# Gated linear attention before a mixture of experts: chunk steps for all head pairs at once, three fp32r passes for the query-key products

## The chip, the cores and the metric

One core of a Trainium2 chip runs the kernel. The metric is the device time of one execution in microseconds (us).

## The reference

Three stages follow each other. The inputs are random; N = 4 * 768 = 3072 tokens, 8 heads of 48 channels, 4 experts.

```python
f = 1 / (1 + exp(-f_logit))                              # [4, 8, 768, 48]
for t in range(768):
    state = f[:, :, t, :, None] * state + k_t (outer) v_t   # per head 48 x 48
    y[:, :, t] = q_t @ state
x = y as [3072, 384]
out = sum over e of p[:, e] * (relu(x @ w1[e]) @ w2[e])     # 384 -> 1024 -> 384
result = ((out @ u1) * (out @ u2)) @ u3 @ uo               # 384 -> 1024 -> 1024 -> 384
```

## The kernel before

The recurrence is computed in chunks of C = 128 tokens. Inside a chunk a running product of 1 + exp(-f_logit), `pi`, is made by a scan; the key is multiplied by `pi`, the query by its reciprocal `r`, and then attention within the chunk is an ordinary masked product, to which the query times the `state` carried from earlier chunks is added. Heads go in NP = 4 pairs; a pair fills R = 96 partitions (48 channels of one head above 48 of the other).

The elementwise part, called prep here (`attn_f` to `attn_q`, L204 to L252), works on one pair and NB = 384 tokens at a time: clamp (L207), exp (L211), add 1 (L218, or L213 on ScalarE for the first four), three scans of 128 columns (L222), ln and exp for the reciprocal (L233, L234), two VectorE instructions that refine it (L241, L242), key and query products on GpSimd (L236, L247). GpSimd also makes `qb` (L258), the query once for each head of a pair with the other head's rows zeroed, so that one matmul over 96 rows gives both heads.

The tensor part, `attn_s` (L273), takes one slot, which is one chunk of one pair; there are 96 slots. TensorE does a transpose of k (L287), the query-key product of 256 columns (L288), the state update `u` (L295) and two or three products for y (L299, L300, L302), all in plain fp32, where a matmul is two passes; the profile counts each pass as an instruction. y leaves TensorE with channels on partitions and is split into a high fp32r part (ScalarE, L334) and the rest (VectorE, L336) in `x`. Slot k does the query-key part of slot k and the y part of slot k - 1.

The expert stage works in units: one expert, one block of 512 tokens, 128 hidden columns. `stage1` is 9 fp32r matmuls (L642), ScalarE and VectorE split their result into high and low (`hid`, L648, L649), and `stage2` is 9 more matmuls (L676) of the unit before. Weights are loaded in chunks of 768 columns and split by `split_chunk` (ScalarE L168, GpSimd L169). The first block's units come in halves of 256 tokens: units 0 to 7 need the first two chunks of attention, units 8 to 15 the first four. A last part (kind "M") does the gated product stage with the same two lines.

The order of everything is written out: each attention step has a due time, the list is sorted, steps up to the eighth slot run before the first unit (that is two chunks, `K0`), and `spread` lays the others over the units by planned time; within a unit the first half of its steps is issued after `stage1` and the other half after `stage2`. Every engine runs its instructions in that order. Loads are issued on SP's queue in the same order.

Of the kernel before, what the change touches and what calls it, by code (L numbers as in the profile page):

```python
# [24 lines left out]
def gated_linear_attention_moe_kernel(  # L25
# [21 lines left out]
    NB = 384  # L47
# [10 lines left out]
    CB = TB // C  # L58

# [10 lines left out]
    fp = ctx.enter_context(tc.tile_pool(name="fp", bufs=3))  # L70
    kqp = ctx.enter_context(tc.tile_pool(name="kqp", bufs=6))
    vtp = ctx.enter_context(tc.tile_pool(name="vtp", bufs=3))
    atp = ctx.enter_context(tc.tile_pool(name="atp", bufs=3))
    qbp = ctx.enter_context(tc.tile_pool(name="qbp", bufs=3))
# [4 lines left out]
    ps_a = ctx.enter_context(tc.tile_pool(name="ps_a", bufs=3, space=PSUM))  # L79
# [19 lines left out]
    def setup():  # L99
# [3 lines left out]
        nc.vector.memset(capt, CAP)  # L103
        nc.vector.memset(cmask, 1.0)
# [9 lines left out]
        nc.vector.tensor_scalar(  # L114
            out=hm[:, 1:2], in0=hm[:, 0:1], scalar1=-1.0, scalar2=1.0, op0=ALU.mult, op1=ALU.add
# [3 lines left out]
    def gate_load():  # L119
        t = const.tile([128, NTILE, E], F32, name="praw")  # L120
        nc.scalar.dma_start(out=t, in_=probs)
        return t
# [8 lines left out]
    def gate_rows(t):  # L131
        ps = ps_a.tile([128, 512], F32, tag="at", name="pT")
# [121 lines left out]
    def attn_b(n, c):  # L254
# [783 lines left out]
```

## Time and profile before

| | |
|---|---|
| median of 3 runs | 1332.62 us (1332.45 to 1333.32) |
| the profiled execution's own time | 1333.76 us |
| its span from first to last instruction | 1332.0 us |
| TensorE / VectorE / ScalarE / GpSimd busy | 1291.6 / 706.3 / 458.8 / 606.0 us |
| mean granted TensorE clock | 0.987 of 2.4 GHz |
| matmuls of the expert and the gated stage (L642, L676) | 41% and 34% of the chain that ended last |
| first attention matmul / first expert matmul / first of unit 8 | 22.95 / 37.00 / 87.90 us from the start |

Busy time counts an instruction from its start to its end; TensorE instructions overlap, so what one costs is the distance from its start to the next one's start. In the profile's names PE is TensorE, PEld its weight load, DVE VectorE, ACT ScalarE, POOL GpSimd.

### The profile page before, as it was taken

What the parts mean: (1) busy time and instruction counts of PE and PEld (TensorE: products, weight loads), DVE (VectorE), ACT (ScalarE), POOL (GpSimd) and SP (SyncE); (2) the same over time, 40 slices, a digit from 0 to 9 for tenths busy, and PEclk for the clock granted to TensorE, in tenths of its full rate; (3) what the DMA queues carried; (4) which work ended last, traced back from release to release, by engine and by line L of the source; (5) the groups of instructions that cost most, each with busy time, mean ns of one, the idle gap of its engine ahead of it and who ended that gap; (6) DMA issues with size and microseconds to landing.
All of it is one profiled execution on the core that took longest, in us unless ns stands there. A gap on an engine that the chain in (4) does not pass through costs nothing.

```text
span 1332.0 us, 17861 instructions
## 1 busy us (share of the span) xinstructions
PE 1291.6 (97%) x6579; PEld 1125.9 (85%) x6579; DVE 706.3 (53%) x1365; ACT 458.8 (34%) x946; POOL 606.0 (45%) x573
## 2 busy tenths in 40 slices
PE   7689999999999999999999999999999999999997
PEld 6588888888887888888788878878888999999997
DVE  6765545445546766665634776767733233332422
ACT  4434424333332423323222332323323334433431
POOL 6656736575354444636354353635625132233310
PEclk8889999999999999999999999999999999999999
DMA  6424224323133252424032241333313323241301
GB/s 190 150 65 143 92 56 145 101 73 112 65 108 126 80 147 77 134 78 143 26 112 103 78 130 53 109 103 97 95 49 118 102 78 113 73 130 55 113 1 39
DMA packets 75584, 128.49 MB, mean 96 GB/s; under 512 B 6528, under 2 KB 48992, under 8 KB 75488
## 3 DMA queue, kind: packets, MB, share of 16 engines
q1 hardware_dynamic: 75344, 127.21, 30.8%
q8 instruction: 54, 0.88, 0.3%
q14 instruction: 42, 0.34, 0.1%
q10 hardware_dynamic: 144, 0.05, 0.0%
HBM read 113.03 MB, written 14.20 MB: 96 GB/s over the span
## 4 chain that ended last, share of the span: by engine, by line
PE 86%; DVE 7%; POOL 2%; issue 2%; ACT 2%; DMA 1%; SPq 0%; POOLq 0%; ACTq 0%; DVEq 0%
PE hps L642 41%; PE y L676 34%; PE psP L288 3%; PE wps L555 2%; PE psQ L299 1%; PE psQ L300 1%; PE psQ L302 1%; DVE pi L222 1%; PE psP L295 1%; POOL acc L696 1%; DVE hid L649 1%; DMA f<-in_fkq_dram 1%; DVE dexp L474 1%; POOL w L169 1%; DVE dexp L473 1%
## 5 line engine op out<-in xcount | busy, mean ns | idle before, releaser
L642 PE MATMUL hps<-x,w 128*128 128x512 f32 (+2 forms) x2952 | 647.4, 366 | 2.6 <-ACT x L334 1.4
L642 PEld LDWEIGHTS hps<-x,w 128*128 128x128 f32 x2952 | 529.4, 189 | 73.0 <-ACT x L334 1.8
L676 PE MATMUL y<-hid,w 128*128 128x512 f32 (+1 forms) x1800 | 445.4, 391 | 10.9 <-DVE hid L649 5.8
L169 POOL TENSOR_TENSOR w<-raw,w 128x768 fp32r<-128x768 f32 x160 | 299.0, 1870 | 263.3 <-ACT w L168 243.6
L676 PEld LDWEIGHTS y<-hid,w 128*128 128x128 f32 x1800 | 329.2, 191 | 82.6 <-DVE hid L649 8.9
L649 DVE SCALAR_TENSOR_TENSOR hid<-hps,hid 128x512 fp32r<-128x512 f32 (+1 forms) x200 | 133.5, 668 | 331.1 <-ACT hid L648 330.7
L648 ACT ACTIVATE hid<-hps 128x512 fp32r<-128x512 f32 (+1 forms) x200 | 115.4, 577 | 293.7 <-PE hps L642 285.1
L168 ACT ACTIVATE w<-raw 128x768 fp32r<-128x768 f32 x160 | 133.9, 837 | 34.4 <-PE y L676 30.7
L656 DVE TENSOR_TENSOR ab<-hps,a 128x384 f32<-128x384 f32 x64 | 35.6, 556 | 164.2 <-PE hps L642 164.2
L493 POOL TENSOR_TENSOR dman<-dman,dexp 128x384 f32<-128x384 f32 (+1 forms) x46 | 46.1, 1003 | 161.2 <-ACT dman L491 154.8
L676 PE MATMUL y<-w,hid 128*128 128x384 f32 x576 | 112.1, 338 | 0.1
L676 PEld LDWEIGHTS y<-w,hid 128*128 128x128 f32 x576 | 101.7, 188 | 0.5 <-DVE hid L658 0.4
L696 POOL TENSOR_TENSOR acc<-acc,tmp 128x512 f32<-128x512 f32 x54 | 70.1, 1326 | 60.7 <-DVE tmp L695 60.7
L340 POOL TENSOR_TENSOR state<-us,pwe 96x96 f32<-96x96 f32 x80 | 28.5, 357 | 127.4 <-DVE us L308 66.5
L491 ACT ACTIVATE dman<-dman 128x384 f32<-128x384 f32 (+1 forms) x46 | 23.9, 520 | 145.8 <-DVE dman L490 130.1
L657 ACT ACTIVATE hid<-ab 128x384 fp32r<-128x384 f32 x64 | 33.6, 525 | 114.9 <-DVE ab L656 114.9
L288 PE MATMUL psP<-qb,kq 96*128 96x256 f32 x180 | 56.5, 396 | 5.2 <-POOL state L340 3.9
L258 POOL TENSOR_TENSOR qb<-kq,hm 96x256 f32<-96x256 f32 x90 | 57.4, 641 | 5.0 <-PE psP L288 5.0
L312 ACT ACTIVATE kT<-psQ 128x96 f32<-128x96 f32 x80 | 19.9, 248 | 111.5 <-PE psQ L302 79.2
L655 ACT ACTIVATE a<-hps 128x384 f32<-128x384 f32 x64 | 31.4, 490 | 77.9 <-PE hps L642 77.2
L336 DVE TENSOR_TENSOR x<-psQ,x 96x128 fp32r<-96x128 f32 (+1 forms) x144 | 41.0, 285 | 28.2 <-ACT x L334 26.9
L658 DVE TENSOR_TENSOR hid<-ab,hid 128x384 fp32r<-128x384 f32 x64 | 35.7, 558 | 37.8 <-ACT hid L657 37.8
(92 smaller groups left out, 1147.8 us busy)
## 6 DMA issues: line engine op xcount, KB each, us to landing
raw<-in_w_dram SPq DMA_DIRECT2D x112, 384.0 KB, 4.2
raw<-in_u_dram SPq DMA_DIRECT2D x27, 384.0 KB, 4.0
kq<-in_fkq_dram SPq DMA_DIRECT2D x30, 288.0 KB, 4.1
vt<-in_vp_dram SPq DMA_DIRECT2D x24, 288.0 KB, 3.1
pb<-pdr SPq DMA_DIRECT2D x24, 256.0 KB, 5.2
raw<-u1d SPq DMA_DIRECT2D x16, 384.0 KB, 3.5
raw<-u2d SPq DMA_DIRECT2D x16, 384.0 KB, 3.6
raw<-wdr SPq DMA_DIRECT2D x16, 384.0 KB, 3.9
```

Source lines behind the costliest of these rows:

```text
L168: nc.scalar.activation(out=w[:, 0], in_=raw, func=AF.Copy)
L169: nc.gpsimd.tensor_tensor(out=w[:, 1], in0=raw, in1=w[:, 0].bitcast(F32), op=ALU.subtract)
L258: nc.gpsimd.tensor_tensor(out=qb, in0=q.unsqueeze(1).to_broadcast([R, 2, C]), in1=hm.unsqueeze(2).to_broadcast([R, 2, C]), op=ALU.mult,)
L288: nc.tensor.matmul(psa, lhsT=kq[:, 0, cs], rhs=at.pop((n, "qb", c)), start=True, stop=True)
L336: nc.vector.tensor_tensor(out=xs[:, 1], in0=ys, in1=xs[:, 0].bitcast(F32), op=ALU.subtract)
L493: nc.gpsimd.tensor_tensor(out=out, in0=s, in1=t.bitcast(F32), op=ALU.mult)
L642: nc.tensor.matmul(ps, lhsT=w[:, wl, j, fs], rhs=x[:, xl, j, t0:t1], start=(n == 0), stop=(n == 3 * KD - 1))
L648: nc.scalar.activation(out=h[:, 0], in_=prods[0], func=AF.Relu)
L649: nc.vector.scalar_tensor_tensor(out=h[:, 1], in0=prods[0], scalar=0.0, in1=h[:, 0].bitcast(F32), op0=ALU.max, op1=ALU.subtract)
L658: nc.vector.tensor_tensor(out=h[:, 1], in0=ab, in1=h[:, 0].bitcast(F32), op=ALU.subtract)
L676: nc.tensor.matmul(yps[t], lhsT=lhsT, rhs=rhs, start=(f == f0 and n == 0), stop=(f == f1 and n == 2))
L696: nc.gpsimd.tensor_tensor(out=at_, in0=at_, in1=tmp, op=ALU.add)
```

## The change

All attention steps now work on one chunk of 128 tokens for all four pairs. A pair's two heads lie on partitions 0 to 47 and 64 to 111 of RP = 112 (rows 48 to 63 are filled with a second copy of channels that a mask removes). The clamp before exp becomes a minimum fused with the addition of 1. The four scans of a chunk are one scan of 516 columns, with a column between pairs that resets the product. Key and query together are split into a high fp32r part (`a_hi`, ScalarE) and a low part (`a_lo`, VectorE for the first eight chunks, GpSimd after that), and the query-key product is three fp32r passes per head over 48 rows: 24 matmuls of 128 columns per chunk in place of four fp32 ones of 256 columns; `qb` is gone. y is summed with tokens on partitions (`a_y`) and three transposes (`a_x`) turn it back. PSUM tiles of attention have three fixed banks. Per chunk there are two loads for f and four for k and q, in pieces of 512 bytes.

```diff
-    kqp = ctx.enter_context(tc.tile_pool(name="kqp", bufs=6))
+    kqp = ctx.enter_context(tc.tile_pool(name="kqp", bufs=3))
...
-    ps_a = ctx.enter_context(tc.tile_pool(name="ps_a", bufs=3, space=PSUM))
+    ps_a = ctx.enter_context(tc.tile_pool(name="ps_a", bufs=1, space=PSUM))
...
+    kqs, vts, at = {}, {}, {}
+    xt = {}
+    XS = (0, 1, 2, 3, 0, 1)
+    ROWS = ((0, 64, 0), (64, RP, D))
+    def where(m):
+        return (m // (S // C), m % (S // C) * C)
+    def load_f(m):
+        b, s0 = where(m)
+        for r0, r1, i in ROWS:
+            nc.sync.dma_start(
+                out=fts[m % 2][r0:r1, :, 1:1 + C],
+                in_=fkq[b, :, i:i + r1 - r0, 0, s0:s0 + C].rearrange("p r t -> r p t"),
+            )
+    def load_kq(m):
+        b, s0 = where(m)
+        t = kqp.tile([RP, NP, 2, C], F32, tag="kq", name="kq")
+        for r0, r1, i in ROWS:
+            for j in range(2):
+                nc.sync.dma_start(
+                    out=t[r0:r1, :, j],
+                    in_=fkq[b, :, i:i + r1 - r0, 1 + j, s0:s0 + C].rearrange("p r t -> r p t"),
+                )
+        kqs[m] = t
+        vts[m] = t
+    ALL = (0, NP)
+    def part(m, key, shape, g, **k):
+        if (m, key) not in at:
+            at[m, key] = atp.tile(shape, name=key, tag=key, **k)
+        return at[m, key][:, g[0]:g[1]]
+    def a_exp(m, g=ALL):
+        f = fts[m % 2][:, g[0]:g[1], 1:]
+    def a_add(m, g=ALL):
+        f = fts[m % 2][:, g[0]:g[1], 1:]
+        nc.vector.tensor_scalar(out=f, in0=f, scalar1=BIG, scalar2=1.0, op0=ALU.min, op1=ALU.add)
+    def a_scan(m, g=ALL):
+        pi = part(m, "pi", [RP, NP, 1 + C], g, dtype=F32)
+        nc.vector.tensor_tensor_scan(
+            out=pi.rearrange("p n t -> p (n t)"), data0=fts[m % 2][:, g[0]:g[1]].rearrange("p n t -> p (n t)"),
+            data1=capt[:, g[0]:g[1]].rearrange("p n t -> p (n t)"), initial=1.0, op0=ALU.mult, op1=ALU.min,
+        )
+    def a_ln(m, g=ALL):
+        pi = part(m, "pi", None, g)
+        r = part(m, "r", [RP, NP, C], g, dtype=F32)
+        nc.scalar.activation(out=r, in_=pi[:, :, 1:], func=AF.Ln)
+        k = kqs[m][:, g[0]:g[1], 0]
+        nc.gpsimd.tensor_tensor(out=k, in0=k, in1=pi[:, :, 1:], op=ALU.mult)
+        nc.gpsimd.tensor_copy(out=pends[:, m, g[0]:g[1]].unsqueeze(2), in_=pi[:, :, C:])
+    def a_rec(m, g=ALL):
+        r = part(m, "r", None, g)
+    def a_newton(m, g=ALL):
+        pi, r = part(m, "pi", None, g)[:, :, 1:], part(m, "r", None, g)
+    def a_q(m, g=ALL):
+        r, q = part(m, "r", None, g), kqs[m][:, g[0]:g[1], 1]
+        eng = nc.vector if m < 2 else nc.gpsimd
+        n = g[1] - g[0]
+            out=pwe[:, m % 3, g[0]:g[1]], in0=r[:, :, C - 1:].to_broadcast([RP, n, 2]),
+            in1=hm.unsqueeze(1).to_broadcast([RP, n, 2]), op=ALU.mult,
+        )
+    def a_hi(m, g=ALL):
+        if (m, "hl") not in at:
+            at[m, "hl"] = atp.tile([RP, 2, NP, 2, C], F32R, tag="hl", name="hl")
+        nc.scalar.activation(out=at[m, "hl"][:, 0, g[0]:g[1]], in_=kqs[m][:, g[0]:g[1]], func=AF.Copy)
+    def a_lo(m, g=ALL):
+        hl = at[m, "hl"]
+        eng = nc.vector if m < 8 else nc.gpsimd
+        eng.tensor_tensor(
+            out=hl[:, 1, g[0]:g[1]], in0=kqs[m][:, g[0]:g[1]], in1=hl[:, 0, g[0]:g[1]].bitcast(F32),
+            op=ALU.subtract,
+        )
+    def last(m):
+        return m % (S // C) == S // C - 1
+    def first(m):
+        return m % (S // C) == 0
+    def bank(m, which):
+        if m < 2 and which in "kyx":
+            return ps_y.tile([128, 512], F32, tag=f"y{'kyx'.index(which)}", name="ps" + which)
+        tag = {"0": "A", "1": "B", "k": "C", "y": "A", "x": "B"}[which]
+        return ps_a.tile([128, 512], F32, tag=tag, name="ps" + which)
+    def a_p(m):
+        hl, kq = at.pop((m, "hl")), kqs[m]
+        if not last(m):
+            ps = bank(m, "k")[:, 0:NP * RP].rearrange("p (n r) -> p n r", n=NP)
+            for p in range(NP):
+                nc.tensor.transpose(ps[:, p], kq[:, p, 0], ident[0:RP, 0:RP])
+            kT = atp.tile([128, NP, RP], F32, tag="kT", name="kT")
+            nc.scalar.activation(out=kT, in_=ps, func=AF.Copy)
+            at[m, "kT"] = kT
+        pp = [bank(m, str(h)).rearrange("p (n t) -> p n t", n=NP) for h in range(2)]
+        for p in range(NP):
+            for n, (kl, ql) in enumerate(PASSES):
+                for h in range(2):
+                    rs = slice(64 * h, 64 * h + D)
+                    nc.tensor.matmul(
+                        pp[h][:, p], lhsT=hl[rs, kl, p, 0], rhs=hl[rs, ql, p, 1], start=(n == 0), stop=(n == 2)
+                    )
+        asb = atp.tile([128, 2, NP, C], F32, tag="asb", name="asb")
+        for h in range(2):
+            nc.vector.tensor_tensor(
+                out=asb[:, h], in0=pp[h], in1=cmask.unsqueeze(1).to_broadcast([128, NP, C]), op=ALU.mult
+            )
+        at[m, "a"] = asb
+    def a_y(m):
+        asb, kq, vt = at.pop((m, "a")), kqs.pop(m), vts[m]
+        ps = bank(m, "y")[:, 0:NP * R].rearrange("p (n r) -> p n r", n=NP)
+        for p in range(NP):
+            if not first(m):
+                nc.tensor.matmul(ps[:, p], lhsT=kq[:, p, 1], rhs=state[:, p], start=True, stop=False)
+            for h in range(2):
+                nc.tensor.matmul(
+                    ps[:, p, h * D:(h + 1) * D], lhsT=asb[:, h, p], rhs=vt[:, p, 2 * h * D:(2 * h + 1) * D],
+                    start=(first(m) and h == 0), stop=(h == 1),
+                )
+        yt = atp.tile([128, KD, C], F32, tag="yt", name="yt")
+        nc.scalar.activation(out=yt[:, :, 0:R], in_=ps[:, 0:KD], func=AF.Copy)
+        nc.scalar.activation(
+            out=yt[:, :, R:C], in_=ps[:, KD].rearrange("p (j r) -> p j r", j=KD), func=AF.Copy
+        )
+        at[m, "yt"] = yt
+    def a_u(m):
+        if last(m):
+            vts.pop(m)
+            return
+        kT, vt = at.pop((m, "kT")), vts.pop(m)
+        ps = bank(m, "k")[0:RP, 0:NP * R].rearrange("p (n r) -> p n r", n=NP)
+        for p in range(NP):
+            nc.tensor.matmul(
+                ps[:, p].rearrange("p (h d) -> p h d", h=2), lhsT=kT[:, p],
+                rhs=vt[:, p].rearrange("p (h d) -> p h d", d=D)[:, 0:3:2], start=True, stop=True,
+            )
+        us = atp.tile([RP, NP, R], F32, tag="kT", name="us")
+        if first(m):
+            nc.vector.tensor_copy(out=us, in_=ps)
+        else:
+            nc.vector.tensor_tensor(out=us, in0=ps, in1=state, op=ALU.add)
+            out=state.rearrange("p n (h d) -> p (n h) d", h=2), in0=us.rearrange("p n (h d) -> p (n h) d", h=2),
+            in1=pwe[:, m % 3].rearrange("p n h -> p (n h)").unsqueeze(2).to_broadcast([RP, 2 * NP, D]), op=ALU.mult,
+        )
+    def a_x(m):
+        b, i = divmod(m, CB)
+        if b not in xt:
+            xt[b] = xp.tile([128, 2, KD, TB], F32R, tag=f"x{XS[b]}", name="x")
+        x = xt[b][:, :, :, i * C:(i + 1) * C]
+        yt = at.pop((m, "yt"))
+        ps = bank(m, "x")[:, 0:KD * C].rearrange("p (j t) -> p j t", j=KD)
+        for j in range(KD):
+            nc.tensor.transpose(ps[:, j], yt[:, j], ident)
+        nc.scalar.activation(out=x[:, 0], in_=ps, func=AF.Copy)
+        nc.vector.tensor_tensor(out=x[:, 1], in0=ps, in1=x[:, 0].bitcast(F32), op=ALU.subtract)
...
+    K0 = 2
+    G0, G1 = (0, 2), (2, 4)
+    asteps = [
+        (a_exp, 0, G0), (a_exp, 0, G1), (a_add, 0, G0), (a_scan, 0, G0), (a_add, 0, G1), (a_ln, 0, G0),
+        (a_scan, 0, G1), (a_rec, 0, G0), (a_exp, 1), (a_newton, 0, G0), (a_ln, 0, G1), (a_q, 0, G0),
+        (a_rec, 0, G1), (a_hi, 0, G0), (a_newton, 0, G1), (a_lo, 0, G0), (a_q, 0, G1), (a_hi, 0, G1),
+        (load_f, 2), (a_add, 1), (a_lo, 0, G1), (a_scan, 1, G0), (a_p, 0), (a_ln, 1, G0), (a_scan, 1, G1),
+        (a_rec, 1, G0), (a_ln, 1, G1), (a_y, 0), (a_newton, 1, G0), (a_rec, 1, G1), (a_q, 1, G0), (a_u, 0),
+        (a_hi, 1, G0), (a_newton, 1, G1), (a_lo, 1, G0), (a_q, 1, G1), (a_x, 0), (a_hi, 1, G1), (a_lo, 1, G1),
+        (a_p, 1), (load_f, 3), (load_kq, 3), (a_exp, 2), (a_y, 1), (a_u, 1), (a_x, 1), (attn_done, 1),
+    ]
+    for m in range(2, NCH):
+        lead = min(1.75, 0.95 + 0.2 * (m - 2))
+        chain = [(a_exp, m), (a_add, m), (a_scan, m), (a_ln, m), (a_rec, m), (a_newton, m), (a_q, m)]
+        for i, st in enumerate(chain):
+            if (st[0], m) != (a_exp, 2):
+                due.append((m - lead + 0.08 * i, st))
+        t = max(m - lead + 0.56, m - 1 + 0.05)
+        due += [(t, (a_hi, m)), (t + 0.1, (a_lo, m))]
+        due += [(m, (a_p, m)), (m + 0.35, (a_y, m)), (m + 0.5, (a_u, m)), (m + 0.75, (a_x, m))]
+        due.append((m + 0.76, (attn_done, m)))
+        if m > 3:
+            due += [(m - 2 - min(1.75, 0.95 + 0.2 * (m - 4)) + 0.2, (load_f, m)), (m - 3 + 0.4, (load_kq, m))]
+        if m > 2:
+            due.append((max(m - 3 + 0.55, 1), (load_v, m)))
+    due.sort(key=lambda d: d[0])
+    asteps += [st for _, st in due]
+    def steps_to(m):
+        return 1 + asteps.index((attn_done, m - 1))
...
-            wb = WB if i > 15 else WB - 1
+            wb = WB
```

## Rows read from the trace of the kernel before

**Rows 1.** Page, busy time by engine
```profile
PE 1291.6 (97%) x6579; PEld 1125.9 (85%) x6579; DVE 706.3 (53%) x1365; ACT 458.8 (34%) x946; POOL 606.0 (45%) x573
```

**Rows 2.** Page, the chain that ended last, shares by line
```profile
PE hps L642 41%; PE y L676 34%; PE psP L288 3%; PE wps L555 2%; PE psQ L299 1%; PE psQ L300 1%; PE psQ L302 1%; DVE pi L222 1%; PE psP L295 1%; POOL acc L696 1%; DVE hid L649 1%; DMA f<-in_fkq_dram 1%; DVE dexp L474 1%; POOL w L169 1%; DVE dexp L473 1%
```

**Rows 3.** Busy time by stretch (count), then granted clock, DMA share, GB/s
```profile
37.00:88.00 51.00, 36.64 (x224) 32.82 (x224) 37.50 (x75) 18.36 (x48) 32.01 (x41) 0.80 0.25 80
88.00:730.00 642.00, 638.46 (x3185) 530.42 (x3186) 358.93 (x754) 222.34 (x483) 334.73 (x346) 1.00 0.33 103
...
50.00:78.00 28.00, 15.86 (x89) 14.38 (x89) 27.46 (x42) 10.58 (x23) 19.85 (x21) 0.71 0.37 118
```

**Rows 4.** Timeline of TensorE: start us, duration, line, tiles, forms
```profile
37.00 2.28 PE L642 MATMUL hps<-x,w 128*128 128x256 f32 x9 [0.69 <-ACT x L334]
...
87.90 2.27 PE L642 MATMUL hps<-x,w 128*128 128x256 f32 x9 [0.68 <-ACT x L334]
```

**Rows 5.** VectorE's groups of instructions from 50 to 78 us
```profile
L222 DVE TENSOR_TENSOR_SCAN pi<-f,capt 96x128 f32<-96x128 f32 x12 | 10.7, 947 | 0.1
L242 DVE SCALAR_TENSOR_TENSOR r<-pi,r 96x384 f32<-96x384 f32 x4 | 5.0, 1249 | 0.1
...
L207 DVE TENSOR_SCALAR f<-f 96x384 f32<-96x384 f32 x4 | 3.2, 801 | 0.0
```

**Rows 6.** Timeline of VectorE from 50 to 78 us
```profile
51.24 0.34 DVE L218 TENSOR_SCALAR f<-f 96x384 f32<-96x384 f32 x1
51.62 1.05 DVE L222 TENSOR_TENSOR_SCAN pi<-f,capt 96x128 f32<-96x128 f32 x3
...
64.89 0.55 DVE L242 SCALAR_TENSOR_TENSOR r<-pi,r 96x384 f32<-96x384 f32 x1
...
70.25 0.41 DVE L649 SCALAR_TENSOR_TENSOR hid<-hps,hid 128x256 fp32r<-128x256 f32 x1
...
73.42 3.34 DVE L242 SCALAR_TENSOR_TENSOR r<-pi,r 96x384 f32<-96x384 f32 x1
```

**Rows 7.** Timeline of GpSimd from 72 to 78 us
```profile
71.96 1.01 POOL L247 TENSOR_TENSOR kq<-kq,r 96x384 f32<-96x384 f32 x1 [1.08 <-DVE r L242]
...
73.41 0.61 POOL L258 TENSOR_TENSOR qb<-kq,hm 96x256 f32<-96x256 f32 x1
...
74.55 1.79 POOL L169 TENSOR_TENSOR w<-raw,w 128x768 fp32r<-128x768 f32 x1
```

**Rows 8.** VectorE's groups over the whole span that read PSUM
```profile
L649 DVE SCALAR_TENSOR_TENSOR hid<-hps,hid 128x512 fp32r<-128x512 f32 x184 | 126.8, 689 | 322.3 <-ACT hid L648 322.0
...
L656 DVE TENSOR_TENSOR ab<-hps,a 128x384 f32<-128x384 f32 x64 | 35.6, 556 | 164.2 <-PE hps L642 164.2
```

**Rows 9.** Timeline of TensorE, one slot among the units
```profile
262.87 0.25 PE L287 MATMUL psQ<-ident,kq 96*128 96x96 f32 x1
262.95 0.62 PE L288 MATMUL psP<-qb,kq 96*128 96x256 f32 x2
263.41 0.33 PE L295 MATMUL psP<-vt,kT 128*96 128x96 f32 x2
263.58 0.38 PE L299 MATMUL psQ<-asb,vt 128*96 128x128 f32 x2
263.80 0.38 PE L300 MATMUL psQ<-asb,vt 128*96 128x128 f32 x2
...
268.42 2.26 PE L676 MATMUL y<-hid,w 128*128 128x512 f32 x9
270.52 0.25 PE L287 MATMUL psQ<-ident,kq 96*128 96x96 f32 x1
```

**Rows 10.** Weight loads of the same slot
```profile
262.87 0.30 PEld L288 LDWEIGHTS psP<-qb,kq 96*128 96x128 f32 x2
```

**Rows 11.** Timeline of TensorE, units of 256 columns
```profile
46.64 1.24 PE L676 MATMUL y<-hid,w 128*128 128x256 f32 x9
47.71 1.23 PE L642 MATMUL hps<-x,w 128*128 128x256 f32 x9
```

More of the change, by code (lines that the diff above doesn't have):

```diff
@@ L103, in setup @@
         nc.vector.memset(capt, CAP)
+        nc.vector.memset(capt[:, :, 0:1], 1.0)
+        for t in fts:
+            nc.vector.memset(t[:, :, 0:1], LIM)
         nc.vector.memset(cmask, 1.0)
@@ L113, in setup @@
         )
[L114 to L115 removed]
+        nc.gpsimd.affine_select(
+            out=hm[:, 1:2], in_=hm[:, 1:2], pattern=[[0, 1]], compare_op=ALU.is_ge,
+            fill=0.0, base=-64, channel_multiplier=1,
         )
     def gate_load():
[L120 removed]
+        t = two.tile([128, NB], F32, tag="d0", name="praw")[:, 0:NTILE * E].rearrange("p (i e) -> p i e", e=E)
         nc.scalar.dma_start(out=t, in_=probs)
@@ L230, in attn_k @@
-    def attn_k(n):
-        pi, k = at[n, "pi"], rq[n][:, 0]
-        r = two.tile([R, NB], F32, tag="r", name="r")
-        nc.scalar.activation(out=r, in_=pi, func=AF.Ln)
+        vts[m] = t
[6 more added lines that the diff above has]
+        f = fts[m % 2][:, g[0]:g[1], 1:]
+        nc.scalar.activation(out=f, in_=f, func=AF.Exp, scale=-1.0)
@@ L416, in gated_linear_attention_moe_kernel @@
-    ready = {st[0][1]: t for t, _, st in due if st[0][0] is attn_q}
-    for k in range(NSLOT):
-        hb, c, p, n, last, first = where(k)
-        t = shifted(k) if k >= NP else k - 12
-        due.append((max(t - 2.7, ready[n] + 0.01) if k >= NP else ready[n] + 0.01, 9, [(attn_b, n, c)]))
-        if k == PER:
-            due.append((k, 10, [(attn_s, k, None, k - 1)]))
-            due.append((t + 0.1, 10, [(attn_s, k, k, None)]))
-        else:
-            due.append((t, 10, [(attn_s, k, k, k - 1 if k else None)]))
-        if p == 0 and k // NP + 2 < NHB * NC_:
-            due.append((t + 1, 11, [(load_v, k // NP + 2)]))
-        if k % (CB * NP) == 1 and k > 1:
-            due.append((t + 0.5, 12, [(attn_n, k // (CB * NP) - 1)]))
@@ L777, in gated_linear_attention_moe_kernel @@
         pr = gate_load()
-        for n in range(NP):
-            load_f(n)
-            load_kq(n)
+        load_f(0)
+        load_kq(0)
+        load_f(1)
+        load_v(0)
+        load_kq(1)
         setup()
-        load_v(0)
         load_v(1)
+        load_kq(2)
+        load_v(2)
         warm(20)
         for i, st in enumerate(asteps[:steps_to(K0)]):
-            if st[0][0] is attn_s and st[0][1] == 0:
+            if st == (a_p, 0):
+                gate_rows(pr)
                 warm(20)
             run(st)
-            if i == 12:
+            if st == (a_newton, 0, G1):
                 gate(pr)
-            if i == 20:
-                gate_rows(pr)
-            if st[0][0] is attn_s and st[0][1] in (5, 6, 7):
+            if st in ((a_p, 0), (a_y, 0), (a_p, 1)):
                 feed(0, 1)
```

207 lines of the change are left out of this document (19 added, 188 removed).

## The prediction

> **What bounds the kernel now.** I read the page first. TensorE is busy for 97% of the span [rows 1], and the chain that ended last runs mostly through the two matmul lines of the units [rows 2]: the kernel is as long as TensorE's instructions and their holes. Then the busy time by stretch, to find the holes. From 88 to 730 us TensorE is busy for 638.46 of 642 us at full clock; there a microsecond less of attention matmuls is a microsecond less of time. From 37 to 88 us it is different: TensorE is busy for 36.64 of 51 us at a granted clock of 0.80 [rows 3]. That stretch begins with the first unit and ends with unit 8 [rows 4], which needs the fourth chunk.
>
> What holds that stretch up is seen from 50 to 78 us, where VectorE is busy for 27.46 of 28 us and GpSimd for 19.85 [rows 3]. Much of VectorE's time is waiting inside its instructions. L242 takes 0.55 us at 64.89 but 3.34 at 73.42 [rows 6], and in those 3.34 us GpSimd runs without a break until 76.34 [rows 7]. Three scans take 1.05 us undisturbed [rows 6], but the twelve scans of the stretch 10.7 [rows 5]. The unit's own L649 reads PSUM and keeps its 0.41 us. Undisturbed, the stretch would need twelve scans of 0.35, eight instructions of 0.55 (L241, L242), eight of 0.35 (L207, L218), 0.7 of copies and 3.4 of PSUM readers, 15.5 us in all [rows 5, 6]. The other 12 us are waiting: 0.6 us for each microsecond of GpSimd. The Trainium skill (SBUF — State Buffer, Who interferes with whom) goes further: an instruction of either engine that needs the shared port pair holds it to its end, and the other blocks fully. The 3.34 us agree with that; over the stretch the trace shows 0.6, not 1.
>
> **What the change costs and saves on TensorE.** Before, by distances between starts in one slot [rows 9]: transpose 0.08, query-key 0.46, u 0.17, each y product 0.22. Eighty slots have a transpose and a u, 80 a state product, all 96 the rest: 80 * (0.08 + 0.17 + 0.22) + 96 * (0.46 + 2 * 0.22) = 124.0 us.
>
> After, per chunk:
> - Four transposes of 112 columns: 4 * 0.08 * 112/96 = 0.37.
> - Four u and four state products of 96 columns: 8 * 0.17 = 1.36.
> - Three transposes back, 128 columns: 3 * 0.107 = 0.32.
> - 24 query-key passes of 128 columns. No fp32r matmul that narrow is in the trace. At 512 columns nine take 2.10 us, 0.233 each [rows 9]; at 256 nine take 1.07, 0.119 each [rows 11]; the line through both gives 0.062 at 128. It could be the weight load that counts: the 128 columns for L288 begin to load at 262.87 [rows 10] and its matmul starts at 262.95, so a load needs at most 0.08. Between 0.062 and 0.08 I take 0.07: 1.68.
> - Eight products of the masked tile with v, 48 columns, two passes each. The stream of a pass is half that of 96 columns, 0.0425, the load again at most 0.08; I take 0.07 a pass: 1.12.
>
> Twenty chunks have the transposes of k and the u, twenty the state product, all 24 the rest: 20 * (0.37 + 0.68 + 0.68) + 24 * (0.32 + 1.68 + 1.12) = 109.5 us, 14.5 less. Four chunks lie ahead of 88 us, where TensorE isn't the bound, so 20/24 count: 12 us. With both prices at 0.08 the sum is 119.1, and the gain 4 us; at the low ends (0.062 and 0.0425) it is 94.3, and the gain 25 us.
>
> The Trainium skill (TensorE: Matmul & The Clock Gate, Back-to-back issue gap) gives about 81 ns for a matmul of 128 columns with its load in a stream, which would cost 5 us of these 12. The same place gives 131 ns for 512 columns, where this trace has 233, so the trace's line is kept.
>
> **The first two chunks.** VectorE's work for them, by width: two adds of 512 columns (0.45 each), scans of 516 (1.41), refinements (2 * 0.73), query products (0.73), low parts of 1,024 (1.47), together 11.0; masks, us and the low part of x read PSUM, 2 * (2 * 0.69 + 0.56 + 0.56) = 5.0 [rows 6, 8]. GpSimd has two key products (1.35), two states (about 1.0 each), three weight splits of 1.79 and small ones, 11 us by [rows 7], and 0.6 of that is 6.6. Together 22.6 us; the steps of a chunk also wait for each other (scan, ScalarE, refinement, product, split, matmul, mask). The first unit can begin between 28 us, if VectorE never idles, and 38. Nearer to the second, because chunk 0 is a chain: I take 35 instead of 37.0 [rows 4].
>
> **Units 0 to 7, to the fourth chunk.** The written order puts there the rest of the chains of chunks 2 to 4, the first half of chunk 5's, and the tensor parts of 2 and 3. VectorE: four adds and scans, three refinements and low parts, 4 * 0.45 + 4 * 1.41 + 3 * 1.47 + 3 * 1.47 = 16.2, and from PSUM eight hid and two sets of masks, us and x, 3.3 + 5.0 = 8.3; 24.5 in all. GpSimd: eight splits 14.4, four key and three query products 9.5, two states and small ones 4.2, 28. With 0.6 of that the stretch is 24.5 + 16.8 = 41 us, where it was 51. Unit 8 then starts at 35 + 41 = 76 instead of 87.9: 12 us, the first two of them from the paragraph above. TensorE's own work sets the lower bound, eight units of 2.15 and two chunks of under 5: 27 us, unit 8 at 62. The upper bound is no gain, 88.
>
> By the skill's full blocking, the 16.2 and the 28 would not overlap at all and unit 8 would start at 35 + 44 = 79.
>
> **After that.** Prep needs less of VectorE than before (qb, clamps and the many small instructions are gone), but its instructions are longer: a scan of 1.41 us, a low part of 1.47. They stand in VectorE's queue ahead of hid (L649), for which stage2 waits, and a stage1 of 2.1 us is the cover. I cost this at nothing, because from 88 to 730 us all holes together are 3.5 us [rows 3] with instructions that wait up to 3.3 us inside VectorE; if the cover fails, see the third rival. SP issues seven loads per chunk where it issued about four, behind waits for the scan and the matmuls that free their tiles; the weight loads queued behind them are three chunks ahead. The 512-byte pieces carry 17% more bytes for f, k and q, on DMA engines that are busy for a third of the time [rows 3]. I cost both at nothing too; were the first loads late, the start would move within the bounds above.
>
> **Sum.** The profiled execution took 1333.76 us: minus 12 ahead of unit 8, minus 12 on TensorE, 1309.8. The median of the runs is 1.1 us below that execution, so I predict 1309.
>
> **Rivals.**
> - *Row halves overlap.* The two heads of a pair sit on different row halves of the array and write different banks; if both stream at once, a pair of query-key passes costs what one does. Then they take 24 * 12 * 0.07 = 20.2 instead of 40.3 us, and 20/24 of the difference is 17 us more gain: 1292. For it: nothing before uses half of the rows, so nothing speaks against it. Against it: the two weight loads remain, and if these run one after the other at up to 0.08 the gain is gone. The Trainium skill (TensorE: Matmul & The Clock Gate, Part 3: Packing small matmuls) says that matmuls in different row groups run concurrently; no row here can show it. Chance 0.16.
> - *Narrow passes don't hide their weight load* (the other side). At 128 and 48 columns load and stream follow each other: 0.08 + 0.062 = 0.142 for each of 24 passes and 0.08 + 0.0425 = 0.12 for each of 16. That is 24 * 0.072 + 16 * 0.05 = 2.5 us more per chunk, 51 us over twenty: 1360. It decides from 0.10 us per narrow pass: 40 passes * 0.03 * 20 is the whole gain of 24 us. For it: every fp32r pass of the trace has 256 columns or more, and their stream covers any load of 0.08. Against it: the passes of u (0.085 for 96 columns) show no added load. Chance 0.14.
> - *Long steps make hid late.* If each chunk makes stage2 wait for one blocked scan or low part beyond its cover, 1.2 us for each of twenty chunks, 24 us: 1333, no change. For it: 3.34 us in one blocked instruction [rows 6]. Against it: only 3.5 us of holes in 642 before. Chance 0.08.
>
> **How the numbers follow.** The forecast has 0.62; its own range is 1292 to 1328 (unit 8 from 68 to 84 us, 4 to 25 us on TensorE, hardly both at one end). The rest of the chance is with the rivals. From 1286 to 1338 lie the forecast, the overlap and the late hid; the unhidden load and some of the overlap's lower bounds stay out, under 0.2. A measurement can tell 0.2%, 2.7 us, from no change. Faster: 0.61 and 0.16, 0.77. Same: most of the third rival and the forecast's edge, 0.07. Slower: 0.14 and what is left, 0.16.
>
> **What would show it.** First unit at about 35 us, first of unit 8 at 76; granted clock below 1 only ahead of that. The distance between starts of query-key passes at 0.07 us, of the 48-column products at 0.14. VectorE's scans at 1.4 us alone and several us beside GpSimd instructions. From there on TensorE without holes, some 0.6 us less per chunk. The prediction is wrong if narrow passes take 0.10 us or more, if unit 8 starts at 88 or later, or if waits of L676 for hid sum to more than some 10 us.

## The result and the profile after

The changed kernel took 1348.62 us in the median of four runs (1346.79 to 1352.12); before took 1332.53 beside it (1330.92 to 1333.32). The ratio is 1.0125, 95% interval 1.0102 to 1.0149: slower by 16 us, where 23.6 less were predicted. The profiled execution, 1346.79 us, has a span of 1345.1, 13.1 more than before, and the account below is made on spans.

The page's busy time by engine and its chain by line, after:

```profile
PE 1307.7 (97%) x7035; PEld 1144.6 (85%) x7035; DVE 645.8 (48%) x1007; ACT 457.2 (34%) x817; POOL 574.1 (43%) x435
...
PE hps L644 41%; PE y L678 34%; PE psy L324 3%; PE ps L306 3%; PE wps L557 2%; PE psy L322 1%; PE psk L343 1%; DMA raw<-in_w_dram 1%; POOL acc L698 1%; DVE dexp L476 1%; POOL w L174 1%; DVE dexp L475 1%; DVE r L253 0%; SPq L201 0%; DVE pi L
```

The bound is where it was [rows 1, 2]: TensorE and its holes. It runs 456 instructions more and is busy for 16 us more, while VectorE has 60 us less and GpSimd 32.

TensorE's timeline at four places: the first unit, the end of chunk 1's tensor part and the query-key passes of chunk 2, and unit 8.

```profile
40.15 4.21 PE L644 MATMUL hps<-x,w 128*128 128x256 f32 x18 [0.58 <-ACT x L367]
...
46.83 0.55 PE L297 MATMUL psk<-ident,kq 112*128 112x112 f32 x4
52.68 0.47 PE L306 MATMUL ps<-hl 48*128 48x128 f32 x2 [5.30 <-ACT hl L268]
...
84.13 1.10 PE L644 MATMUL hps<-x,w 128*128 128x256 f32 x5 [0.56 <-ACT x L367]
```

These answer to [rows 4]. The span divides so (the work on either side of unit 8 differs by less than a chunk):

| stretch | before | predicted | after |
|---|---|---|---|
| start to first unit | 37.0 | 35 (-2) | 40.15 (+3.2) |
| first unit to unit 8 | 50.9 | 41 (-10) | 43.98 (-6.9) |
| unit 8 to the end | 1244.1 | 1232 (-12) | 1260.97 (+16.9) |

So the stretches ahead of unit 8 gave 3.8 us instead of 12, and the rest lost 16.9 instead of gaining 12. For the last row I summed, line by line, the distance from each TensorE instruction's start to the next one's, behind 87.90 us before and 84.13 after (the last group of the span, which has no next one, is left out):

```
                                     before   after
attention without holes                96.3   105.3   +9.0
  of it query-key passes L306                  32.0   (39.2 less holes of 7.2)
  heads' products L324                         32.6
  state products L322                          16.6
  u L343, kT L297, x back L366                 24.1
holes ahead of the query-key products   0.2     7.2   +7.0
units (L642 and L676, L644 and L678) 1101.4  1102.6   +1.2
```

TensorE's own attention work grew, and it now has holes. The waits of TensorE over the whole span, by line and releaser (total, times, longest), show the holes:

```profile
PE ps L306 <- DVE x L368: 8.1, 4, 4.7
PE ps L306 <- ACT hl L268: 5.3, 1, 5.3
```

The first lie at 69.60, 114.42, 163.45 and 413.39 us, the second is the wait of chunk 2 above. Busy time by stretch then shows what comes with holes (length, busy time of TensorE, its weight loads, VectorE, ScalarE, GpSimd; granted clock, DMA share, GB/s):

```profile
40.15:84.13 43.98, 35.24 (x261) 33.94 (x261) 26.06 (x34) 19.45 (x37) 25.34 (x23) 0.82 0.43 122
...
24.00:28.00 4.00, 2.05 (x10) 1.22 (x8) 3.97 (x5) 1.09 (x3) 3.09 (x4) 0.50 0.73 182
32.00:36.00 4.00, 3.89 (x18) 3.65 (x17) 0.80 (x2) 0.00 (x0) 0.43 (x1) 0.50 0.01 3
...
150.00:200.00 50.00, 48.90 (x267) 40.51 (x266) 21.44 (x29) 14.11 (x24) 17.12 (x17) 0.97 0.18 52
400.00:450.00 50.00, 45.27 (x239) 37.56 (x238) 27.80 (x41) 12.84 (x23) 18.96 (x16) 0.90 0.28 88
```

The first line is the stretch from the first unit to unit 8, to which the first of [rows 3] answers. The clock is at its lower level (1.2 GHz, 0.50) from 21.4 to 45.3 us. It fell again at 52.2 us, inside the wait of chunk 2, and at 76.1. Behind unit 8 it fell at 164.8, behind the hole that ends at 163.45, for 3.4 us, and at 410.6, inside the hole that ends at 413.39, until 420.8. Chunk 0's first matmul began at 16.86 us, 6 us earlier than before; the first unit still came 3.2 us later.

### The profile page after: what moved, and what is told of

It reads as the page before. It is cut to its first block, busy times and chain, and to the rows that moved or that the text cites. A ratio compares the mean times of both kernels' runs of the same rounds, so it can differ in the third digit from the quotient of the medians.

```text
span 1345.1 us, 18234 instructions
## 1 busy us (share of the span) xinstructions
PE 1307.7 (97%) x7035; PEld 1144.6 (85%) x7035; DVE 645.8 (48%) x1007; ACT 457.2 (34%) x817; POOL 574.1 (43%) x435
## 4 chain that ended last, share of the span: by engine, by line
PE 86%; DVE 6%; issue 2%; POOL 2%; ACT 1%; DMA 1%; SPq 1%; POOLq 0%; ACTq 0%; DVEq 0%
PE hps L644 41%; PE y L678 34%; PE psy L324 3%; PE ps L306 3%; PE wps L557 2%; PE psy L322 1%; PE psk L343 1%; DMA raw<-in_w_dram 1%; POOL acc L698 1%; DVE dexp L476 1%; POOL w L174 1%; DVE dexp L475 1%; DVE r L253 0%; SPq L201 0%; DVE pi L252 0%
## 5 line engine op out<-in xcount | busy, mean ns | idle before, releaser
L174 POOL TENSOR_TENSOR w<-raw,w 128x768 fp32r<-128x768 f32 x160 | 303.0, 1896 | 307.0 <-ACT w L173 280.8
L493 ACT ACTIVATE dman<-dman 128x384 f32<-128x384 f32 (+1 forms) x46 | 24.0, 521 | 143.7 <-DVE dman L492 139.0
L273 POOL TENSOR_TENSOR hl<-kq,hl 112x1024 fp32r<-112x1024 f32 x16 | 39.9, 2493 | 43.1 <-ACT hl L268 43.1
L306 PE MATMUL ps<-hl 48*128 48x128 f32 x576 | 43.2, 294 | 14.9 <-DVE x L368 8.1
L324 PE MATMUL psy<-vt,asb 128*128 128x48 f32 x384 | 56.2, 275 | 1.1 <-DVE asb L311 1.0
L306 PEld LDWEIGHTS ps<-hl 48*128 48x128 f32 x576 | 38.5, 204 | 20.5 <-DVE x L368 8.7
L324 PEld LDWEIGHTS psy<-vt,asb 128*128 128x128 f32 x384 | 52.5, 199 | 2.0 <-DVE asb L311 1.6
```

The costliest lines, as they stand in the source:

```text
L174: nc.gpsimd.tensor_tensor(out=w[:, 1], in0=raw, in1=w[:, 0].bitcast(F32), op=ALU.subtract)
L273: eng.tensor_tensor(out=hl[:, 1, g[0]:g[1]], in0=kqs[m][:, g[0]:g[1]], in1=hl[:, 0, g[0]:g[1]].bitcast(F32), op=ALU.subtract,)
L306: nc.tensor.matmul(pp[h][:, p], lhsT=hl[rs, kl, p, 0], rhs=hl[rs, ql, p, 1], start=(n == 0), stop=(n == 2))
L324: nc.tensor.matmul(ps[:, p, h * D:(h + 1) * D], lhsT=asb[:, h, p], rhs=vt[:, p, 2 * h * D:(2 * h + 1) * D], start=(first(m) and h == 0), s ...
```

## The experiments

**What a narrow pass costs.** TensorE's timeline of one undisturbed chunk, its y part and later its query-key part:

```profile
267.73 0.36 PE L322 MATMUL psy<-state,kq 112*128 112x96 f32 x2
267.92 0.57 PE L324 MATMUL psy<-vt,asb 128*128 128x48 f32 x4
268.33 0.43 PE L322 MATMUL psy<-state,kq 112*128 112x96 f32 x2
...
290.44 1.55 PE L306 MATMUL ps<-hl 48*128 48x128 f32 x24
291.93 0.96 PE L644 MATMUL hps<-x,w 128*128 128x512 f32 x3
```

Four passes of a pair's heads go from 267.92 to 268.33, 0.10 us each, with 48 columns moving; 24 query-key passes take 1.49, 0.062 each, with 128 moving. The narrower stream is the dearer one. Theory: the load of 128 stationary columns takes about 0.10 us and sets the price of a narrow pass, except in the query-key part, where the passes alternate between row halves.

*e1_wide* makes the stream of the heads' products twice as wide (each head's product fills the pair's 96 channels):

```diff
-ps[:, p, h * D:(h + 1) * D], lhsT=asb[:, h, p], rhs=vt[:, p, 2 * h * D:(2 * h + 1) * D],
+ps[:, p], lhsT=asb[:, h, p], rhs=vt[:, p, h * D:h * D + R],
```

> The eight products of the masked tile with v per chunk get 96 moving columns in place of 48 (the v tile's zero block is used, the output is the same). Theory 1, a pass costs the load of its 128 stationary columns whenever its stream is shorter: the distance between starts stays at 0.10 us a pass, a chunk's y products stay at 2.6 to 2.7 us, and the time stays within 3 us of the changed kernel's 1348.6. Theory 2, the pass costs its stream and a fixed part: 0.0425 us more for each of 16 passes, 0.68 us a chunk, so y at 3.3 us and the kernel some 14 us longer (20 chunks behind unit 8).

It took 1348.35 us in its one execution. TensorE's timeline of the same chunk's y part:

```profile
269.28 0.36 PE L322 MATMUL psy<-state,kq 112*128 112x96 f32 x2
269.48 0.61 PE L324 MATMUL psy<-vt,asb 128*128 128x96 f32 x4
...
271.88 0.94 PE L678 MATMUL y<-hid,w 128*128 128x512 f32 x3
```

The 24 passes took 2.60 us (269.28 to 271.88) where the changed kernel's took 2.59 (267.73 to 270.32), 0.108 each. Twice the stream for nothing: the load is the price, and the stream runs beside it. A fixed price for any pass, whatever its load, would not explain it either: the query-key passes get by with 0.062.

*e2_halves* keeps all query-key passes and only orders them by row half:

```diff
-for p in range(NP):
-    for n, (kl, ql) in enumerate(PASSES):
-        for h in range(2):
+for h in range(2):
+    for p in range(NP):
+        for n, (kl, ql) in enumerate(PASSES):
```

> The 24 query-key passes of a chunk are issued by row half: twelve for the first head rows, then twelve for the second, in place of alternating. Theory 1a, a pass of 128 columns is at 0.062 us because the other half's weights load while one half streams: in a row on one half, load and stream show, a pass comes to 0.10 us or more, a chunk's 24 passes from 1.49 to about 2.5 us, the kernel some 20 us longer. Theory 1b, an fp32r load of 48 rows is simply shorter than the stream: 1.5 us as now, and the time within 3 us of 1348.6.

1374.43 us in its one execution, 26 more than the changed kernel. TensorE's timeline:

```profile
268.22 2.50 PE L306 MATMUL ps<-hl 48*128 48x128 f32 x24
270.66 1.66 PE L678 MATMUL y<-hid,w 128*128 128x512 f32 x6
```

2.44 us for 24 passes, 0.102 each, against 0.062: 0.95 us for each of 24 chunks is 23 of the 26. How the alternating passes save a load is seen from single starts. Query-key passes at work in windows that begin together and end later and later (length, busy time, count, granted clock, DMA share, GB/s), the changed kernel first, then e2:

```profile
290.43:290.60 0.17, 0.16 (x2) 1.00 0.00 0
290.43:290.63 0.20, 0.19 (x4) 1.00 0.00 0
290.43:290.70 0.27, 0.26 (x4) 1.00 0.00 0
290.43:290.74 0.31, 0.30 (x6) 1.00 0.00 0
```

```profile
268.21:268.38 0.17, 0.16 (x1) 1.00 0.00 0
268.21:268.41 0.20, 0.19 (x2) 1.00 0.00 0
268.21:268.49 0.28, 0.27 (x2) 1.00 0.00 0
268.21:268.52 0.31, 0.30 (x3) 1.00 0.00 0
```

In the changed kernel the count grows by two at a time: the two passes of a pair start together (the single records, at 290.607 and 290.608 us, then at 290.716 and 290.721), and so do their loads. In e2 it grows by one, at the same 0.11 us. So within one row half loads follow each other at 0.11 us, whatever streams; the two halves load and stream at the same time, and a pair of passes shares the price of one load.

The Trainium skill (TensorE: Matmul & The Clock Gate, LDWEIGHTS (loading the stationary operand)) makes the load 107 ns for 128 columns, an estimate from its P / 1.2, whatever the rows; the 0.108 of e1's y part with 112 and 128 rows and the 0.102 of e2 with 48 agree. The section Part 3: Packing small matmuls of that page of the Trainium skill says that a load overlaps matmuls in flight only where the row group differs. That the two halves overlap agrees with the traces; the "only" does not: the units' passes of 256 columns, all on the same 128 rows, take 0.119 us each [rows 11], which leaves no room for a load of 0.11 us that is not beside a stream, and in e1 twice the stream cost nothing.

**The holes behind 88 us.** The attention has three PSUM banks, and x shares one with the query-key product of the second heads, so this product of chunk m + 1 has to wait until VectorE's L368 has read x of chunk m. VectorE's timeline ahead of the longest hole, and TensorE's behind it:

```profile
405.44 1.15 DVE L252 SCALAR_TENSOR_TENSOR pi<-pi,r 112x512 f32<-112x512 f32 x1
406.63 1.67 DVE L253 SCALAR_TENSOR_TENSOR r<-pi,r 112x512 f32<-112x512 f32 x1
...
408.88 1.50 DVE L492 SCALAR_TENSOR_TENSOR dman<-dlow,dman 128x384 f32<-128x384 int32 x1
412.18 0.69 DVE L651 SCALAR_TENSOR_TENSOR hid<-hps,hid 128x512 fp32r<-128x512 f32 x1 [1.81 <-ACT hid L650]
412.79 0.55 DVE L368 TENSOR_TENSOR x<-psx,x 128x384 fp32r<-128x384 f32 x1
```

```profile
413.39 2.82 PE L306 MATMUL ps<-hl 48*128 48x128 f32 x23 [4.73 <-DVE x L368]
416.14 4.21 PE L644 MATMUL hps<-x,w 128*128 128x512 f32 x9
420.14 2.10 PE L678 MATMUL y<-hid,w 128*128 128x512 f32 x7
```

L368 is in its place in VectorE's queue behind prep, arithmetic on the weights (L492) and a hid that itself waits 1.81 us for ScalarE. ScalarE's queue does its part: L493, which follows L492, waited there for 7.78 us, with the first half of the split of x (L367) behind it. TensorE stands for 4.73 us. The clock falls to half inside this hole, so the passes behind it take 2.82 instead of 1.55 and a stage1 4.21 instead of 2.25.

*e3_xearly* issues the split of x (L366 to L368) earlier, by its due time alone:

```diff
-(m + 0.75, (a_x, m))]
+(m + 0.56, (a_x, m))]
```

> The step that transposes y back and splits it is due at 0.56 of a chunk in place of 0.75, right after the state update, so ahead of the next chunks' reciprocal, refinement and query product in VectorE's and ScalarE's queues; nothing else changes. Theory 3, the holes of 8.1 us in the query-key passes are the third PSUM bank, which the low part of x still holds because VectorE gets to it late: with the step earlier the waits for it go, and with them the half-clock stretches behind the holes at 163 and 413 us; 8 to 12 us less than the changed kernel, about 1338. Rival, VectorE is late whatever the order: the wait turns up at another line (L678 for hid, or the masks) and the time stays within 3 us.

1334.81 us (1333.65 to 1335.82), ratio to before 1.0016 (1.0006 to 1.0025): 13.8 less than the changed kernel, some more than expected. No wait for L368 is left. Behind unit 8, L306 takes 29.7 us instead of 39.2 and the units 1098.1 instead of 1102.6: the holes gave back 7.2 us, and the instructions behind them, which had run at half clock, most of the other 6.8 (behind unit 8 the clock is full in e3 up to the last 5 us).

**The start.** VectorE's timeline up to the wait of chunk 2:

```profile
39.03 0.56 DVE L351 TENSOR_TENSOR us<-psk,state 112x384 f32<-112x384 f32 x1 [6.24 <-PE psk L343]
...
42.89 0.42 DVE L651 SCALAR_TENSOR_TENSOR hid<-hps,hid 128x256 fp32r<-128x256 f32 x1 [2.20 <-ACT hid L650]
43.23 0.42 DVE L227 TENSOR_SCALAR ft<-ft 112x512 f32<-112x512 f32 x1
43.68 1.23 DVE L232 TENSOR_TENSOR_SCAN pi<-ft,capt 112x516 f32<-112x516 f32 x1
47.34 0.42 DVE L651 SCALAR_TENSOR_TENSOR hid<-hps,hid 128x256 fp32r<-128x256 f32 x1 [2.42 <-ACT hid L650]
47.68 1.79 DVE L252 SCALAR_TENSOR_TENSOR pi<-pi,r 112x512 f32<-112x512 f32 x1
49.51 0.69 DVE L253 SCALAR_TENSOR_TENSOR r<-pi,r 112x512 f32<-112x512 f32 x1
52.66 1.23 DVE L273 TENSOR_TENSOR hl<-kq,hl 112x1024 fp32r<-112x1024 f32 x1 [2.46 <-ACT hl L268]
```

VectorE idles for 6.24 us ahead of its part of chunk 1's u (L351), until TensorE's L343 is done, and the add and scan of chunk 2 (L227, L232) stand in the queue behind it and behind the first unit's hid. Two theories: the half clock makes chunk 1's tensor part long and everything late; or the written order does, because it puts chunk 2's chain behind that idle time.

*e4_warm* (on the changed kernel) and *e7_warm30* (on e3) put matmuls that compute nothing needed into TensorE's holes, to hold the clock up: 8 ahead of `(a_y, 0)`, and 14 or 30 ahead of `(a_p, 1)`.

```diff
+            if st in ((a_y, 0), (a_p, 1)):
+                warm(8 if st[0] is a_y else 14)
```

> Two rows of warm-up matmuls more (128 columns, plain fp32): eight ahead of the y products of chunk 0 and fourteen ahead of the query-key part of chunk 1, where TensorE stood still for 0.8 and 2.5 us; nothing else changes. Theory 4, the first two chunks lost time because the granted clock was at half from 21.7 to 45.5 us: with the clock kept at full the first unit starts at 34 to 36 us in place of 40.15 and unit 8 at 78 to 80 in place of 84.1, the kernel 4 to 7 us shorter. Rival, the chain over VectorE, GpSimd and ScalarE sets the pace there: first unit and unit 8 move by less than 2 us, or the extra matmuls (22 of 0.22 us) delay them.

> On top of the earlier step for x (1334.8 us): eight warm-up matmuls ahead of the y products of chunk 0 and thirty ahead of the query-key part of chunk 1, so that this part runs in one go when its last operand is there. In the run with fourteen the clock fell at 32 us, behind holes in that part, and stayed at half to 45. Theory 4, half clock is what the first two chunks lose: with the clock full to 46 us the first unit starts at 36 to 37 us in place of 39.9 and unit 8 at 79 in place of 82.7, the kernel 3 us shorter. Rival, the chain of chunk 2 decides, whatever the clock: its query-key part still starts at 52 us and the time is within 1.5 us of 1334.8.

e4: 1347.30 us (1346.53 to 1348.86), ratio 1.0108 (1.0091 to 1.0125); full clock to 32 us instead of 21.4, first unit at 39.89, unit 8 at 83.90. e7: 1333.65 us (1332.63 to 1336.15), ratio 1.0013 (1.0003 to 1.0022), not to be told from e3. Full clock to 34.0 us, first unit at 39.88, and chunk 2's query-key part still at 52.40. So 11 to 14 us more of full clock bought at most 0.3 us. But nearly all of chunk 1's y part ran at half clock in both (from 32.1 to 45.8 us and from 34.0 to 44.3); what full clock would save there, neither run shows.

*e8_early2* (on e3) issues chunk 2's add to query product ahead of chunk 1's y part, and its high and low parts on either side of chunk 1's x:

```diff
-(a_exp, 2), (a_y, 1), (a_u, 1), (a_x, 1), (attn_done, 1),
+(a_exp, 2), (a_add, 2), (a_scan, 2), (a_ln, 2), (a_rec, 2), (a_newton, 2),
+(a_q, 2), (a_y, 1), (a_u, 1), (a_hi, 2), (a_x, 1), (a_lo, 2), (attn_done, 1),
...
```

> On top of the earlier step for x (1334.8 us): the prep of chunk 2 is issued ahead of chunk 1's y part, where VectorE stands idle from 32.8 to 39 us, in place of after the first unit's split; nothing else changes. Theory 5, the 5.6 us in which TensorE waits for chunk 2's high part at 47 to 52 us come from the written order, because that chain stands in every queue behind the first units' hid: the wait goes or falls below 1 us, unit 8 starts 5 to 8 us earlier (75 to 78 us in place of 82.7), the kernel about 1328. Rival, the engines' work sets the pace: the wait moves to chunk 3 or to the masks, unit 8 within 2 us of 82.7, the time within 2 us of 1334.8.

The 82.7 which this text and e7's give for unit 8 of e3 was the start of unit 7; unit 8 starts at 84.90 there. 1323.57 us (1322.21 to 1325.86), ratio 0.9939 (0.9923 to 0.9956), 11.2 less than e3. TensorE's timeline, chunk 2's query-key part and unit 8:

```profile
44.58 1.56 PE L306 MATMUL ps<-hl 48*128 48x128 f32 x24
...
72.03 0.52 PE L645 MATMUL hps<-x,w 128*128 128x256 f32 x3
```

The 5.6 us wait for the high part is gone, and unit 8 starts 12.9 us earlier, with the clock still at half from 23.4 to 43.8 us. So the order was the cause of the wait; the first unit, at 40.28, did not move by it.

**y without transposes.** *e5_ychan* (on e3) makes y with channels on partitions: v and the state are the stationary operands (96 columns), 128 tokens move, and x is split straight from PSUM in four pieces.

```diff
-ps[:, p, h * D:(h + 1) * D], lhsT=asb[:, h, p], rhs=vt[:, p, 2 * h * D:(2 * h + 1) * D],
+ps[:, p], lhsT=vt[:, p, h * D:h * D + R], rhs=asb[:, h, p],
...
```

> On top of the earlier step for x (1334.8 us): y is summed by channel again, as in the kernel before, inside the chunk step of four pairs: the v tile (96 columns) and the state are the stationary operands, 128 tokens move, no transposes back; ScalarE and VectorE split y straight from PSUM in four pieces each. Theory 1, y by token gains nothing because a pass of its 128-column weights costs 0.10 to 0.11 us whatever its stream: by channel a pass also costs 0.11, y stays at 2.6 to 2.7 us a chunk and the transposes' 0.25 us go; 5 to 8 us less, about 1328. Rival, the sums by token are the cheaper form and the eight small pieces on ScalarE and VectorE cost more than the transposes: 1335 or more.

1326.66 us (1325.78 to 1329.43), ratio 0.9959 (0.9946 to 0.9971), 8.2 less than e3. The span is 7.2 us shorter: 3.2 ahead of unit 8, which starts at 81.70, and 4.0 behind it. There y takes 48.4 us (heads 34.7, state 13.7); by token it takes 54.2 (32.5, 16.8, transposes 4.9). Sums by token saved nothing, and the transposes came on top; some 2 of these 5.8 us were lost again in the units.

**All together.** *e10_three* is early x, early chunk 2 and y by channel; *e9_warm* is that with 8 and 30 warm matmuls.

> The three edits that shortened the kernel together: x earlier, chunk 2's prep ahead of chunk 1's y part, y summed by channel. If the three costs are separate (the third bank behind VectorE, the order of the first chunks, the transposes back), the gains add: 1334.8 - 11.2 - 8.2 = 1315. Rival, the four pieces by which ScalarE and VectorE split y collide with the earlier prep among the first units: 1319 or more, with waits for hid or for the masks ahead of 90 us.

> As the kernel with the three edits, and the eight and thirty warm-up matmuls ahead of chunk 0's y and chunk 1's query-key part. With y by token and these matmuls the clock still fell inside chunk 1's y part, at 34 us. Theory 4a, it falls there because of the 48-column passes: by channel, with 128 columns a pass, it stays full from 16 us on, the first unit starts at 36 to 37 us in place of 40 and the kernel is 3 us shorter than without them (1312). Rival, it falls there for the holes of some tenths that the masks leave: first unit at 39 to 40, the time within 1.5 us of the kernel without them.

e10: 1322.92 us (1321.83 to 1324.60), ratio 0.9929 (0.9913 to 0.9946), where 1315 was expected. Behind unit 8 it gains on e8 (1244.8 against 1248.5), but unit 8 starts at 76.79 instead of 72.03. One of TensorE's waits, the one ahead of the first unit:

```profile
PE hps L640 <- ACT x L361: 1.6, 1, 1.6
```

e9: 1324.18 us (1323.16 to 1325.24), ratio 0.9936 (0.9919 to 0.9953). The clock stayed full to 43.3 us, which shortened chunk 1's y part, and the first unit came later still. Its timelines of TensorE and ScalarE:

```profile
42.91 1.16 PE L640 MATMUL hps<-x,w 128*128 128x256 f32 x3 [4.56 <-ACT x L361]
```

```profile
41.16 1.06 ACT L268 ACTIVATE hl<-kq 112x1024 fp32r<-112x1024 f32 x1 [2.89 <-POOL kq L258]
42.12 1.33 ACT L361 ACTIVATE x<-psy 96x384 fp32r<-96x384 f32 x4
```

By channel, x of chunk 1 is ready early, but stands in ScalarE's queue behind the high part of chunk 2, which waits for GpSimd. So *e11_mixed* is e8 with y by token for chunks 0 to 3 and by channel from chunk 4, with this condition in the y part and in the split of x:

```diff
...
+        if m < 4:
...
```

> As the kernel with the three edits, but y by token for chunks 0 to 3 and by channel from chunk 4 on. The three edits together start unit 8 at 76.8 us, x earlier and chunk 2's early prep alone at 72.0; behind unit 8 the sums by channel are 3.7 us shorter (1244.8 against 1248.5 us to the end). Theory 6, the pieces of the split cost only among the first units: unit 8 at 72 and 1245 us behind it, a span near 1317 and a time of 1318 to 1320. Rival, the 3.7 us behind unit 8 are the later start's (work already done by then): 1322 to 1324, as both.

1318.18 us (1317.76 to 1320.35), ratio 0.9894 (0.9877 to 0.9910): faster than both kernels, 14.4 us below before and 30 below the changed one. TensorE's timeline at unit 8:

```profile
73.73 0.52 PE L665 MATMUL hps<-x,w 128*128 128x256 f32 x3
```

Behind it the span has 1242.6 us, 5.9 less than e8's; that is e5's gain on y, 54.2 less 48.4.

## Why the prediction was wrong

**What bounds the kernel: right.** TensorE and its holes, before and after.

**A load "needs at most 0.08": the step that failed first.** It was read as the 0.08 us between the start of a load and that of its matmul [rows 9, 10]. That distance bounds nothing: in the changed kernel's y part a matmul starts 0.04 us behind its load (267.951 and 267.992 us) where loads follow each other at 0.11. [Rows 10] has 0.30 for the two loads, and that was not weighed. Of the terms behind unit 8 (20/24 of each term's whole), L324 was to take 22.4 us and took 32.6 (0.10 a pass instead of 0.07), L322 11.3 and took 16.6, L297 6.2 and took 7.7. Together 17 us. The query-key term came out, 33.6 forecast and 32.0 measured, but by luck: its 0.07 stood for the stream or the load of one pass, while what was measured is a load of 0.11 to 0.12 that two passes share; in e2 the same passes cost 0.102. The state product of before was over-priced too: at L302 behind 87.90 us it took 9.6 us for 68 products, 0.14 each, where 0.22 was taken, 5.4 us in all. Without that, attention before was 96.5 us there and not the 103 of my sum.

So the rival of unhidden loads was half right. The load is the price of a narrow pass, but load and stream don't add up: the load alone counts, and in the query-key part two passes share it. The rival of overlapping halves had the mechanism right and the price wrong: the two passes of a pair do start together, but a pair then costs two times 0.062, the price of a load, and not 0.07.

**"I cost this at nothing": the second step that failed.** The cover that I named was stage1 ahead of hid. What was late was the split of x, through a bank that the next chunk's query-key product needs; hid's own waits summed to 2.6 us. e3 prices it: 13.8 us, about half as idle time and about half in what ran behind the holes, most of it at the lower clock. The sum in the third rival, 24 us, was too high and its place another one.

**First unit at 35, unit 8 at 76: missed by 5 and 8 us.** The 41 us between them came to 43.98, but not as summed. VectorE was busy for 26.06 us there and GpSimd for 25.34. With each VectorE instruction at the shortest time that its kind took in this run, the work is 22.3 us, so of the 16.8 us of blocking that I added 4 to 5 are there (L252 above at 1.79 us instead of 0.68 is one of them), 0.2 us for each microsecond of GpSimd and not 0.6. In place of the rest VectorE idles, waiting for its chain. e8 shows that order was the cause: with chunk 2's chain ahead of chunk 1's y part, unit 8 starts at 72.03; the changed kernel's 84.13 was just outside my own bounds of 68 to 84. For the first unit at 40.15 no cause was shown. Half clock in chunk 1's y part is the rival that stands: with u and x behind it, it took from 31.41 to 39.57 us in the changed kernel, and no run had it at full clock with y by token. e4 and e7 lost the clock at 32.1 and 34.0 us, with most of it still to come; e9 kept it, with y by channel, but there ScalarE's queue held x back and the first unit came at 42.91.

**What would make it wrong, as listed:** narrow passes of 0.10 us or more, true for the heads' products; unit 8 at 88 or later, not so; waits for hid, not so, but another hole that the list lacked.

## What to carry to other kernels

Price a narrow matmul by its stationary columns first: with 128 of them it took 0.10 to 0.11 us here, whether 48 or 96 columns moved, and only two passes on different row halves shared that price. When a change gives TensorE a new PSUM bank to wait for, find the reader that frees it and all that stands ahead of that reader in its engine's queue; here the waits cost their idle time and about as much again behind them. An early stretch in which no engine is busy throughout may be bound by the written order of the queues: here moving one late chain forward gave 11.2 us, more than the one saving of work that was tried.

## What the runs showed of the hardware

The granted clock fell while TensorE was almost without holes. Busy time by stretch of e7, then of e9 (length, busy time of TensorE, its weight loads, VectorE, ScalarE, GpSimd; granted clock, DMA share, GB/s):

```profile
28.00:32.00 4.00, 4.00 (x48) 3.79 (x47) 2.19 (x6) 2.14 (x4) 0.73 (x2) 1.00 0.37 131
32.00:36.00 4.00, 3.44 (x20) 3.15 (x20) 1.21 (x2) 0.29 (x1) 1.66 (x1) 0.75 0.00 0
36.00:40.00 4.00, 3.42 (x18) 3.02 (x17) 0.70 (x2) 1.22 (x4) 0.53 (x1) 0.50 0.00 0
```

```profile
32.00:36.00 4.00, 3.08 (x37) 2.72 (x37) 2.38 (x4) 1.79 (x3) 1.82 (x1) 1.00 0.02 6
36.00:40.00 4.00, 2.36 (x23) 2.19 (x21) 2.49 (x4) 1.26 (x2) 1.46 (x3) 1.00 0.22 64
```

In e7 it fell at 34.0 us, inside chunk 1's y part by token, after 4 us without a hole and then holes of 0.39 and 0.18 us only. In e9, with y by channel and with more idle time (busy for 2.36 of 4 us), it stayed there, and fell at 43.3 us, behind a hole of 4.56. e9 also has chunk 2's chain earlier, so the two differ in more than the form of y; what makes the difference was not tried. And where the clock stayed up longer it bought nothing: e7 and e9 were no faster than the same kernels without warm matmuls.
